# Head-by-head value loads, sums by head pair, and dummy products in the start of a fused attention and gated feed-forward kernel

## The chip, the cores and the metric

One core of one Trainium2 chip. The metric is the time of one execution on the device in microseconds (us), the median of several runs. A profiled run also gives the span, from the first to the last instruction that the trace holds; it is 1.7 us shorter than the run's time in most runs, and up to 2.6 us in a few. PE is the TensorE matrix engine, DVE is VectorE, ACT is ScalarE, POOL is GpSimd; "PEld" is PE's weight load. The granted clock of PE is 1.00 at full rate and 0.50 at half rate; in these traces it takes only these two values, so anything between is an average over a stretch.

Every ratio below is the mean time of one kernel's fast runs over that of the kernel before in the same rounds, so it is not quite the ratio of the medians quoted beside it.

## The reference

```python
batch, n_heads, seq, head_dim = 4, 8, 768, 64
k_sum = k.reshape(B, H, 24, 32, D).max(axis=3)       # one key for each block of 32
v_sum = v.reshape(B, H, 24, 32, D).mean(axis=3)      # one value for each block
# softmax over: keys nearer than 16 positions, and the 24 block keys (+ log 32)
x = softmax_scores @ concat(v, v_sum)                # -> 3072 tokens x 512
g = x @ w_gate                                       # 512 x 1536
ffn = (gelu(g) * (x @ w_val)) @ w_out
out = x + sigmoid(x @ w_res) * ffn
```

## The kernel before: the parts that the change touches

The work is cut into eight units (half a batch element each, 384 tokens). A unit computes scores (`s_step`: PE products, Exp on ACT, mask on DVE), value products (`av_step`: PE, reciprocal and scaling on DVE), transposes (`xt_step`: PE, copy on ACT or DVE), then twelve pairs of gate and value products (`fo_step`: PE, Gelu on ACT, product on DVE), then the output (`res_step`, `ffn_step`, `end_step`). The attention of unit u+1 is woven into the output of unit u, so only the attention of unit 0 has nothing to hide behind. The instruction order on each engine is the order of the program.

`vext` holds the values: rows 0 to 95 a window of positions, rows 96 to 127 the block means, which are products with an averaging matrix.

```python
def v_loads(b):                       # 12 loads, one window of all 8 heads each
    for t in range(NT):
        r0, r1, src = v_window(b, t)
        nc.gpsimd.dma_start(out=vext[b % 2][r0:r1, t, :, 0:D], in_=src)
# ... setup, k, q and v loads, then at once all weight loads on POOL's queue ...

for hp in range(3):
    k_step(0, hp, ps_mm, "mm")
# ... fourth key pair, first two query pairs
s_step(0, 0, st)
q_step(0, 0, 2, ps_mm, "mm")
vsum_mm(0, vs, 0, 3)                  # block means of ALL heads, window by window
s_step(0, 1, st)
# ... s_step 2 and 3, vsum_mm up to NT
nc.vector.tensor_copy(vsum[0][96:128, 0:DM // 2], vs[0][96:128, 0:DM // 2])
# ... copies of the means into vext on DVE, ACT, POOL
keep_warm(2)                          # dummy 128x128 products, 512 columns
av_step(0, 0, st)
keep_warm(2)
av_step(0, 1, st, ps_mm, "mm")
# ... xt_step and av_step in turn
g0, v0 = mm_tile("g"), mm_tile("vv")
gv_mm(g0, w_gate, st, 0, (0, 1))      # gate/value products begin
# ...
gv_end(gvT, 0, g0, v0)                # first Gelu

for u in range(NU):
    for fo in range(0 if u else 2, FO):
        fo_step(st, gvT, fo)
        if u == 0 and fo >= 8:
            q_step(0, 1, fo - 8, ps_t, "t")
        if u == 0 and fo == 10:       # first Exp of unit 1, amid the Gelus of unit 0
            nst = new_unit()
            s_step(1, 0, nst)
    # ... first_out: output of unit 0 with the rest of unit 1's attention
```

The softmax here doesn't subtract the row's maximum and nothing guards it: scores larger than these inputs give would overflow.

## Time and profile before

| | before |
|---|---|
| time, median of its first 3 runs | 282.56 us |
| span of the profiled run | 281.2 us |
| PE busy | 260.4 us, 93% |
| first keys landed, PE starts | 6.4 us |
| first value product | 21.55 us |
| steady gate/value products from | 29.36 us |
| first product of unit 1 | 60.60 us |

The page of the profile: the span, PE's busy time, and the busy share of PE in 40 slices of 7 us, in tenths.

```profile
span 281.2 us, 5757 instructions
...
PE   0799996999999999999899999999899999999994
...
PE 83%; DVE 6%; ACT 4%; issue 3%; DMA 3%; POOL 0%; POOLq 0%; DVEq 0%
```

The last line is the chain of work that ended last, by engine. PE is the limit nearly everywhere. A change that leaves PE's work alone can gain in the first two slices and in slice 7, where PE is not full, and wherever PE is full only because it runs at half rate, which this page does not show.

The timeline of the start of the kernel before (start, duration, engine, line, operation, what is written and read, how many; in brackets the idle time before and who ended it):

```profile
13.07 1.46 PE L241 MATMUL vs<-vext,bmat 96*32 96x256 bf16 x6
...
20.77 1.00 DVE L247 COPY vext<-vsum 32x768 bf16<-32x768 bf16 x2
...
21.55 0.54 PE L294 MATMUL ao<-vext,P 128*64 128x65 bf16 x12
...
25.23 0.42 PE L294 MATMUL ao<-vext,P 128*64 128x65 bf16 x12
...
27.53 1.28 ACT L321 ACT_TABLE_LOAD   x1
...
28.82 0.87 ACT L321 ACTIVATE ge<-g 128x384 f32<-128x384 f32 x2
...
29.36 0.81 PE L316 MATMUL g<-xT,w_gate 128*128 128x384 bf16 x4 [0.42 <-ACT ge L321]
```

The means are built over 7 us and copied before the first value product. Twelve value products take 0.54 us, and from 25.2 us on 0.42 and then 0.38: PE ran at half rate until about 25 us.

The same view of the middle, where the first Exp of unit 1 stands among the Gelus of unit 0:

```profile
42.85 1.28 ACT L280 ACT_TABLE_LOAD   x1
...
44.14 0.90 ACT L280 ACTIVATE P<-s,bias_t 128x768 bf16<-128x768 f32 x1
45.06 1.28 ACT L321 ACT_TABLE_LOAD   x1
...
45.09 0.35 PE L276 MATMUL s<-qT,kW 64*128 64x64 bf16 x12 [0.81 <-ACT P L280]
...
47.23 1.28 ACT L280 ACT_TABLE_LOAD   x1
...
49.48 0.35 PE L276 MATMUL s<-qT,kW 64*128 64x64 bf16 x12 [1.89 <-ACT P L280]
```

ACT loads the Exp table, the Gelu table and the Exp table again, and PE waits 0.81 and 1.89 us for it.

### The profile page before, as it was taken

How to read it: one execution, taken by the hardware profiler on the slowest of the kernel's cores; microseconds unless marked ns; L12 is line 12 of the kernel's file. 1: busy time of each engine (PE TensorE's matmuls, PEld its weight loads, DVE VectorE, ACT ScalarE, POOL GpSimd, SP SyncE). 2: the span in 40 equal slices, each digit the busy share in tenths (PEclk: the TensorE clock that was granted, in tenths of full speed). 3: DMA queues.
4: the chain of work that ended last, by engine and by line, in shares of the span. 5: the costliest groups of instructions: out<-in, count | busy, mean ns of one | idle time of the engine just before them, and what ended most of it. 6: DMA issues, size and time to landing. Idle time of an engine off the chain costs nothing.

```text
span 281.2 us, 5757 instructions
## 1 busy us (share of the span) xinstructions
PE 260.4 (93%) x2326; PEld 144.2 (51%) x2349; DVE 163.5 (58%) x366; ACT 131.9 (47%) x205; POOL 103.3 (37%) x130
## 2 busy tenths in 40 slices
PE   0799996999999999999899999999899999999994
PEld 0555553455555556455454555455455555456543
DVE  5965432489636734486866834575956733684424
ACT  1855549556473553652353434543254435444320
POOL 7995753600199982000899830000700000000000
PEclk9999999999999999999999999999999999999999
DMA  6999999991019999961099999421001100010003
GB/s 89 171 178 196 197 206 208 151 198 54 4 10 127 182 171 152 151 98 65 3 100 131 196 166 150 94 77 41 2 0 40 75 2 0 37 41 37 2 0 113
DMA packets 99818, 27.51 MB, mean 98 GB/s; under 512 B 83720, under 2 KB 96848, under 8 KB 99792
## 3 DMA queue, kind: packets, MB, share of 16 engines
q0 software_dynamic: 80560, 16.85, 68.4%
q1 hardware_dynamic: 19232, 10.30, 17.1%
q8 instruction: 18, 0.29, 0.4%
q14 instruction: 8, 0.07, 0.1%
HBM read 33.69 MB, written 6.29 MB: 142 GB/s over the span
## 4 chain that ended last, share of the span: by engine, by line
PE 83%; DVE 6%; ACT 4%; issue 3%; DMA 3%; POOL 0%; POOLq 0%; DVEq 0%
PE f L348 21%; PE g L316 20%; PE vv L316 19%; PE r L338 7%; PE ao L294 4%; PE s L276 3%; DMA q_sb<-in_q_dram 3%; PE xp L305 3%; DVE ks L207 2%; PE vs L241 2%; PE tp L233 2%; DVE gvT L322 2%; PE f L369 1%; ACT L280 1%; ACT L321 1%
## 5 line engine op out<-in xcount | busy, mean ns | idle before, releaser
L322 DVE TENSOR_TENSOR gvT<-ge,vv 128x384 bf16<-128x384 f32 x96 | 52.6, 552 | 58.9 <-PE vv L316 54.8
L321 ACT ACTIVATE ge<-g 128x384 f32<-128x384 f32 x96 | 47.0, 491 | 82.2 <-DVE gvT L322 43.7
L316 PE MATMUL vv<-xT,w_val 128*128 128x384 bf16 x384 | 78.4, 326 | 2.7 <-DVE gvT L322 2.7
L316 PE MATMUL g<-xT,w_gate 128*128 128x384 bf16 x384 | 79.9, 326 | 0.4 <-ACT ge L321 0.4
L348 PE MATMUL f<-w_out,gvT 128*128 128x512 bf16 x262 | 62.7, 379 | 1.4 <-issue 1.0
L316 PEld LDWEIGHTS <-w_val 128*128 128x128 bf16 x384 | 37.5, 98 | 28.7 <-issue 4.6
L316 PEld LDWEIGHTS <-w_gate 128*128 128x128 bf16 x384 | 35.8, 98 | 25.2 <-issue 3.0
L266 POOL COPY vext<-vsum 32x1536 bf16<-32x1536 bf16 x14 | 20.0, 1464 | 76.6 <-DMA vsum<-vpart 76.6
L280 ACT ACTIVATE P<-s,bias_t 128x768 bf16<-128x768 f32 x32 | 28.8, 901 | 30.6 <-PE s L276 30.5
L111 POOL DMA_DIRECT2D vext<-in_v_dram x48 | 36.5, 790 | 15.7 <-DMA w_out<-in_moe_w_out_dram 5.4
L348 PEld LDWEIGHTS <-gvT 128*128 128x128 bf16 x276 | 26.1, 98 | 29.1
L283 DVE TENSOR_TENSOR P<-P,maskt 128x768 bf16<-128x768 bf16 x32 | 17.7, 556 | 21.6 <-ACT P L280 21.6
L338 PE MATMUL r<-w_res,xT 128*128 128x512 bf16 x88 | 23.9, 381 | 0.4
L354 DVE SCALAR_TENSOR_TENSOR th<-th,f 128x512 f32<-128x512 f32 (+1 forms) x25 | 16.5, 659 | 6.4 <-PE f L348 6.1
L300 DVE TENSOR_TENSOR xn<-ao,rz 128x384 bf16<-128x384 f32 x32 | 17.8, 558 | 1.1
L119 POOL DMA_DIRECT2D k_nat<-in_k_dram x24 | 18.1, 771 | 0.0
L356 DVE SCALAR_TENSOR_TENSOR o<-th,xn 128x512 f32<-128x512 f32 (+1 forms) x25 | 16.8, 671 | 0.9
L298 DVE RECIPROCAL rz<-ao 128x6 f32<-128x6 f32 x32 | 6.2, 193 | 17.7 <-PE ao L294 17.7
L294 PEld LDWEIGHTS <-P 128*64 128x64 bf16 x384 | 9.0, 115 | 14.1 <-DVE P L283 5.5
L341 ACT ACTIVATE th<-r 128x512 f32<-128x512 f32 x24 | 14.2, 595 | 3.3 <-PE r L338 2.9
L207 DVE TENSOR_REDUCE ks<-kW 128x24 bf16<-128x768 bf16 x16 | 15.2, 948 | 0.3
L276 PE MATMUL s<-qT,kW 64*128 64x64 bf16 x384 | 11.8, 197 | 2.7 <-ACT P L280 2.7
(69 smaller groups left out, 188.4 us busy)
## 6 DMA issues: line engine op xcount, KB each, us to landing
out_dram<-o SPq DMA_DIRECT2D x23, 256.0 KB
vext<-in_v_dram POOLq DMA_DIRECT2D x40, 96.0 KB, 6.0
k_nat<-in_k_dram POOLq DMA_DIRECT2D x20, 96.0 KB, 3.7
q_sb<-in_q_dram POOLq DMA_DIRECT2D x4, 384.0 KB, 7.3
w_gate<-in_moe_w_gate_dram POOLq DMA_DIRECT2D x6, 256.0 KB, 8.2
w_val<-in_moe_w_val_dram POOLq DMA_DIRECT2D x6, 256.0 KB, 9.3
w_out<-in_moe_w_out_dram POOLq DMA_DIRECT2D x3, 512.0 KB, 14.3
q_nat<-in_q_dram POOLq DMA_DIRECT2D x12, 128.0 KB, 5.2
```

What stands on the lines that cost most here:

```text
L111: nc.gpsimd.dma_start(out=vext[b % 2][r0:r1, t, :, 0:D], in_=src)
L119: nc.gpsimd.dma_start(out=k_nat[r0:r0 + hi - lo, t].rearrange("p (h d) -> p h d", d=D), in_=k[b, :, lo:hi, :].rearrange("h p d -> p h d"))
L207: nc.vector.tensor_reduce(out=ks.rearrange("d (t n) -> d t n", n=2), in_=kw[:, :, WIN:WIN + QT].rearrange("d t (n w) -> d t n w", w=BLK), ...
L266: eng.tensor_copy(vext[b % 2][96:128, lo:hi, :, 0:D], src)
L276: nc.tensor.matmul(s[:, hh, t * QT:(t + 1) * QT], kw[ps, tt, hp, :], qt[ps, tt // 2, hp, (tt % 2) * QT:(tt % 2 + 1) * QT], start=True, sto ...
L280: nc.scalar.activation(P.rearrange("p a t q -> p a (t q)"), s[:, :, 0:TU], AF.Exp, scale=scale, bias=bias_t[:])
L294: nc.tensor.matmul(ao[64 * e:64 * e + 64, sub, hh, :], P[:, hh, t, :], vext[b % 2][:, half * HT + t, 2 * hp + hh, 0:D + 1], start=True, st ...
L316: nc.tensor.matmul(ps[:, 0:TU], w[:, ko, fo * 128:(fo + 1) * 128], st["xT"][:, ko, :], start=(ko == 0), stop=(ko == KO - 1), skip_group_ch ...
L321: nc.scalar.activation(ge[:], g[:, 0:TU], AF.Gelu)
L322: nc.vector.tensor_mul(gvT[:, fo, :], ge[:], vv[:, 0:TU])
L338: nc.tensor.matmul(r[:], st["xT"][:, ko, ss], w_res[:, ko, :], start=(ko == 0), stop=(ko == KO - 1))
L348: nc.tensor.matmul(st["f", sub][:], gvT[:, fo, ss], w_out[:, fo, :], start=(fo == 0), stop=(fo == FO - 1), skip_group_check=True)
```

## The change

Its intent: start unit 0's value products per head pair as soon as that pair's values have landed; release PE's clock early by dummy products; take the Gelu table load off the way; and move unit 1's first Exp behind the last Gelu. The diff, cut to its core:

```diff
 def v_loads(b):
-    for t in range(NT):
-        r0, r1, src = v_window(b, t)
-        nc.gpsimd.dma_start(out=vext[b % 2][r0:r1, t, :, 0:D], in_=src)
+    # first and last window for all heads (2 loads, cut here), then
+    for h in range(H):
+        src = bass.AP(tensor=v.tensor, offset=..., ap=[[D, BAND], [QT * D, NT - 2], [1, D]])
+        nc.gpsimd.dma_start(out=dst[0:BAND, 1:NT - 1, h, 0:D], in_=src)
@@ setup
+nc.vector.memset(warm[:], 0.0)            # first of all
-(memsets of vsum[1], bgrp, k_nat, kW[1])  # moved to behind xt_step(0, 2)
-(all weight loads)                        # now chunk by chunk: load_gv(c), load_rest()
+def vsum_pair(hp):
+    vs = ps_t.tile([128, 512], F32, tag="t", name="vs")
+    for t in range(NT):
+        nc.tensor.matmul(vs[96:128, 0:128], bmat[:, t, :], vext[0][0:BAND, t, 2 * hp:2 * hp + 2, 0:D], ...)
+    nc.scalar.copy(vsum[0][96:128, cols], vs[96:128, 0:128])
+    nc.gpsimd.tensor_copy(vext[0][96:128, 0:HT, 2 * hp:2 * hp + 2, 0:D], ...)
@@ start
+keep_warm(12)
 k_step(0, 0), k_step(0, 1)
+keep_warm(3)
 k_step(0, 2), fourth key pair
+keep_warm(4)
 q_step(0, 0, 0)
+keep_warm(2)
 q_step(0, 0, 1); s_step(0, 0); q_step(0, 0, 2); s_step(0, 1); q_step(0, 0, 3)
+vsum_pair(0); load_gv(1)
 s_step(0, 2); av_step(0, 0)
+vsum_pair(1); load_gv(2)
 s_step(0, 3)
+nc.scalar.activation(gate1[:], bias_t[0:1, :], AF.Gelu)     # loads the Gelu table
 xt_step(0, 0); av_step(0, 1)
+vsum_pair(2); load_gv(3)
 xt_step(0, 1); av_step(0, 2)
+vsum_pair(3); load_rest()
 xt_step(0, 2); keep_warm(2)
+(memsets of batch 1)
 gv_mm(g0, w_gate, st, 0, (0, 1)); av_step(0, 3); gv_mm(v0, ...); xt_step(0, 3); ...
@@ unit 0
-if u == 0 and fo == 10:
-    nst = new_unit()
-    s_step(1, 0, nst)
@@ first_out: s_step(n, 0) now leads, and the twelve ffn groups are spread anew (cut)
```

The copy of a sum takes two engines: ACT reads it out of PSUM, POOL spreads it. That follows the Trainium skill, "Trainium Kernel Development and Optimization", Key Constraints: POOL cannot access PSUM.

## The prediction

> **What bounds it now.** The page gives PE 93% busy over 281.2 us and 83% of the chain that ended last. From unit 1 on (60.6 us) PE's work is left alone, so only the first 60.6 us can move.
>
> There, by the timeline:
> - PE starts at 6.4 us, when the first keys land, and runs at half rate until about 25.1 us (12 products of the value step take 0.54 us, then 0.38).
> - Values are summed for all heads at once (PE 13.1 to 20.3 us), then copied into the value tile; the first value product waits until 21.55 us. The first Gelu follows at 28.82 us, behind a table load of 1.28 us; steady gate/value products start at 29.36 us.
> - From 29.36 to 60.60 us PE idles about 2.8 us: 0.81 and 1.89 us at 44.3 and 47.6 us, where unit 1's first Exp costs ScalarE two extra table loads (1.28 us each) amid the Gelus.
>
> By issue plus time to landing (DMA view), value loads land from 11.1 to 18.4 us, the last gate/value weights at 37.2 us, needed at 41.2 us.
>
> **What changes.**
> 1. Block sums, broadcast and value products go by head pair, the broadcast on POOL (32x1536 takes 1.46 us; estimate 0.73 us for a pair). The first value product moves to about 17 us. But each POOL copy stands between two weight issues of 0.77 us, so POOL's order sets the last copy: I estimate starts at 16.1, 18.4, 20.7 and 23.0 us. ScalarE's own chain (four key copies of 0.96, four query copies of 0.48, four Exps of 0.90 us, the query landing unchanged at 10.57) gives nearly the same beat.
> 2. The Gelu table load moves ahead of the transposed copies, off the chain: 1.3 us.
> 3. Setup memsets leave VectorE's early queue: about 1.1 us on its key chain.
> 4. Dummy products around the key transposes: PE warm by about 6.5 us.
> 5. Unit 1's first Exp moves behind the last Gelu: two table loads and 2.7 us of PE idle go; 28.4 us of work remain.
> 6. Value loads: 10 instead of 12, same bytes and 128-byte writes; no change in landing.
>
> **On the critical path.** If PE stays at full rate, gate/value work starts near 26.7 instead of 29.36 (2.6 us), plus 2.7 us from step 5: 5.3 us, unit 1 starting near 55.3. Weights (37.2 against a need at 38.3) still just arrive. That is 277.2 us.
>
> **The doubt.** The Trainium skill, "TensorE: Matmul & The Clock Gate", Part 1, says that a window of about 3.4 us of activity releases the clock and an idle one throttles it again. This trace shows that busy is not enough: from 12.2 to 20.3 us PE was full of small products (64-row, 32-column) and stayed at half rate. Between 11 and 22 us the changed kernel has just such products and no dummies. If the clock falls back there, PE's order becomes the limit (an estimated 2 to 4 us lost), leaving 279.5 to 281.
>
> **Predicted:** 278.0 us, range 276.4 to 281.0. Faster by over 2% 0.25, within 2% 0.73, slower 0.02.
>
> **What would show it.** Right: first value products near 17 us, 12 of them in 0.38 us; gate/value stream from 26 to 27 us; no PE gap over 1 us from 40 to 50 us; unit 1 near 55 us; the later span as before. Wrong: 0.54 us value products at 17 to 24 us (clock fell back); PE waiting on weight DMAs at 33 to 38 us; POOL copies much over 0.8 us.
>
> **Would make it wrong:** the clock state either way; POOL copies starving the weight DMAs; a much faster start, which the weights' arrival caps near 276 us.

## More of the kernel before

Busy time by stretches in the kernel before; the number after POOL's is the mean granted clock of PE:

```profile
core 0: us, PE busy (x) PEld busy (x) DVE busy (x) ACT busy (x) POOL busy (x), PEclk, DMA share, GB/s
15.00:18.40 3.40, 3.40 (x40) 1.99 (x42) 2.20 (x5) 2.17 (x3) 3.40 (x6) 1.00 2.14 166
```

Here one must read with care. The granted clock reads 1.00, but the products in this stretch have their half-rate durations. The clock's record begins only with the first release (at 25.4 us here); before it the column reads full. The durations of like products decide.

## The result, and the profile after

| | before | after |
|---|---|---|
| time, median of 4 runs each | 282.32 us | 281.78 us |
| ratio | | 0.9985 (0.9963 to 1.0006) |
| span of the profiled run | 281.2 us | 279.9 us |
| steady gate/value products from | 29.36 us | 30.05 us |
| first product of unit 1 | 60.60 us | 58.79 us |
| from the steady start to the end of the span | 251.8 us | 249.9 us |

The time is the same. The start is 0.7 us later, not 2.6 earlier, and the rest 1.9 us shorter. The profiled run of before was one of its longer ones (282.86 us against a median of 282.32), so the difference of the spans overstates that of the times.

The page after:

```profile
span 279.9 us, 5851 instructions
...
PE   8778999999999999999899999999899999999994
...
PEclk9965999999999999999999999999999999999999
```

The gap of slice 7 is gone. In slices 3 and 4 the granted clock is 0.6 and 0.5. The stretches:

```profile
core 0: us, PE busy (x) PEld busy (x) DVE busy (x) ACT busy (x) POOL busy (x), PEclk, DMA share, GB/s
13.20:16.60 3.40, 1.85 (x54) 1.61 (x54) 2.28 (x5) 3.11 (x6) 2.64 (x5) 1.00 2.51 155
16.60:20.00 3.40, 3.04 (x52) 2.48 (x48) 1.42 (x4) 1.51 (x3) 2.62 (x4) 0.51 2.07 178
...
23.50:26.90 3.40, 3.40 (x30) 2.03 (x28) 2.02 (x18) 0.74 (x2) 2.49 (x4) 0.50 1.46 195
26.90:30.30 3.40, 2.94 (x25) 1.66 (x22) 1.25 (x3) 1.35 (x3) 3.40 (x6) 1.00 1.44 194
```

The clock was released by the first dummies, fell back at 16.6 us after 3.4 us in which PE was busy only 1.85 us, and stayed at half for 10.2 us (16.65 to 26.89 us by the clock's record). The timeline of the start:

```profile
1.26 5.29 PE L376 MATMUL wp<-warm 128*128 128x512 bf16 x12 [1.26 <-DVE warm L150]
...
14.13 0.84 PE L242 MATMUL vs<-vext,bmat 96*32 96x128 bf16 x12
...
16.44 0.42 PE L293 MATMUL ao<-vext,P 128*64 128x65 bf16 x12 [1.18 <-POOL vext L246]
...
16.79 1.46 PE L242 MATMUL vs<-vext,bmat 96*32 96x128 bf16 x12
...
19.48 0.54 PE L293 MATMUL ao<-vext,P 128*64 128x65 bf16 x12 [0.36 <-POOL vext L246]
...
22.72 0.54 PE L293 MATMUL ao<-vext,P 128*64 128x65 bf16 x12 [0.87 <-POOL vext L246]
...
26.51 0.53 PE L293 MATMUL ao<-vext,P 128*64 128x65 bf16 x12
...
30.05 0.81 PE L315 MATMUL g<-xT,w_gate 128*128 128x384 bf16 x4
```

The first value products come at 16.44 us, 5 us sooner. But the sums of a pair then take 1.46 instead of 0.84 us, and a pair takes over 3 us, so the fourth pair's products come at 26.5 us. The same view further on, where unit 1 is prepared and begins:

```profile
45.24 1.28 ACT L279 ACT_TABLE_LOAD   x1
...
46.65 1.89 PE L347 MATMUL f<-w_out,gvT 128*128 128x512 bf16 x8
...
48.47 0.38 PE L293 MATMUL ao<-vext,P 128*64 128x65 bf16 x12
```

One table load is left, and PE works through it without a gap.

### The profile page after: what moved, and what is told of

Read it like the earlier page. It is cut to its first block, busy times and chain, and to the rows that moved or that the text cites. A ratio compares the mean times of both kernels' runs of the same rounds, so it can differ in the third digit from the quotient of the medians.

```text
span 279.9 us, 5851 instructions
## 1 busy us (share of the span) xinstructions
PE 266.5 (95%) x2391; PEld 146.0 (52%) x2391; DVE 161.7 (58%) x363; ACT 128.8 (46%) x205; POOL 102.0 (36%) x126
## 4 chain that ended last, share of the span: by engine, by line
PE 84%; DVE 5%; ACT 4%; DMA 3%; issue 2%; POOL 1%; POOLq 0%
PE g L315 21%; PE f L347 21%; PE vv L315 20%; PE r L337 8%; PE ao L293 4%; PE s L275 3%; DMA q_sb<-in_q_dram 3%; PE xp L304 2%; DVE ks L207 2%; PE tp L233 1%; DVE gvT L321 1%; ACT P L279 1%; PE vs L242 1%; PE vs L253 1%; PE f L368 1%
## 5 line engine op out<-in xcount | busy, mean ns | idle before, releaser
L347 PE MATMUL f<-w_out,gvT 128*128 128x512 bf16 x276 | 65.5, 379 | 0.0
L279 ACT ACTIVATE P<-s,bias_t 128x768 bf16<-128x768 f32 x32 | 28.9, 902 | 29.9 <-PE s L275 29.7
L111 POOL DMA_DIRECT2D vext<-in_v_dram x32 | 26.3, 854 | 11.1 <-DMA w_out<-in_moe_w_out_dram 5.1
L293 PE MATMUL ao<-vext,P 128*64 128x65 bf16 x384 | 12.7, 203 | 2.4 <-POOL vext L246 2.4
```

The lines of the kernel that those rows point to most:

```text
L111: nc.gpsimd.dma_start(out=dst[0:BAND, 1:NT - 1, h, 0:D], in_=src)
L279: nc.scalar.activation(P.rearrange("p a t q -> p a (t q)"), s[:, :, 0:TU], AF.Exp, scale=scale, bias=bias_t[:])
L293: nc.tensor.matmul(ao[64 * e:64 * e + 64, sub, hh, :], P[:, hh, t, :], vext[b % 2][:, half * HT + t, 2 * hp + hh, 0:D + 1], start=True, st ...
L347: nc.tensor.matmul(st["f", sub][:], gvT[:, fo, ss], w_out[:, fo, :], start=(fo == 0), stop=(fo == FO - 1), skip_group_check=True)
```

## The experiments

Fourteen kernels; all gave the right result. Each is told against the kernel before in the same rounds. The medians of the kernel before were 282.3 to 282.7 us. The changed kernel was not run again in these rounds, so a difference from it, or between kernels of different rounds (e1 to e4, e5 to e8, e9 to e11, e12 to e14), can be off by some tenths of a us.

### e2_second_alone: the second part on the old start

Edit: the kernel before, with the early `s_step(1, 0)` taken out and the new `first_out` put in.

> The kernel before with only the second part of the change: unit 1's first Exp moved behind the last Gelu, and the new order of the output step. If that part is worth what the idle of PE says (2.7 us): about 279.6 us. If, as the trace of the changed kernel suggests, about 0.7 to 1.4 us are given back where unit 1 begins (the last transposed copy comes later and delays the Gelu table load): 280.3 to 281.0 us, with the first 42 us as before.

Measured: 280.03 us, ratio 0.9915 (0.9889 to 0.9941). In the profile, steady start (28.64 us) to end of span takes 249.7 us, against 251.8 before: 2.1 us of gain. It is between the two expectations and slightly nearer the second, so a part of the gain is given back. That start of 28.64 us is 0.7 us earlier than in the profiled run of before, with the same code: the clock was released at 22.9 us here and at 25.4 us there, and the value products take 0.38 us from 22.97 us on here, while they still took 0.54 at 24.33 us there. So the steady start of the changed kernel is 0.7 to 1.4 us later than the old one.

### e3_start_alone: the new start with the old second part

Edit: the changed kernel with the old `first_out` and the early `s_step(1, 0)` put back.

> The changed kernel with the output step and the first Exp of unit 1 put back as before, so only the new start is left. Trace reading: the gate/value stream starts 0.7 us later than before because PE is at half rate from 16.9 to 27.1 us; so slower than before by about 0.5 to 0.9 us (282.8 to 283.2 us). If the start were the gain and the second part the loss: faster than before by 1 us or more.

Measured: 284.57 us, ratio 1.0069 (1.0041 to 1.0097): slower, by more than expected. The steady start is at 29.97 us as in the changed kernel. The surplus is a second fall of the clock, in the old gap. Busy time by stretches of e3_start_alone:

```profile
47.00:50.40 3.40, 1.51 (x30) 0.81 (x28) 0.88 (x2) 3.37 (x5) 0.82 (x1) 1.00 1.34 202
50.40:53.80 3.40, 3.40 (x12) 1.27 (x10) 1.46 (x4) 2.00 (x4) 1.97 (x3) 0.51 2.39 155
```

PE was busy 1.51 of 3.4 us, waiting for the table loads, and the next 3.4 us ran at half rate. If PE is the limit there, that costs about 1.7 us (an estimate: 3.4 x 0.5), which is the size of the surplus. But the same gap in the profiled run of the kernel before, with the same 1.51 us, brought no fall:

```profile
46.80:50.20 3.40, 1.51 (x29) 0.80 (x27) 1.26 (x4) 3.37 (x6) 0.77 (x1) 1.00 1.46 195
50.20:53.60 3.40, 3.40 (x27) 1.54 (x25) 1.07 (x2) 1.48 (x3) 2.21 (x3) 1.00 2.40 154
```

Counted in steps of 3.41 us from the clock's own changes, the emptiest window of that gap has 1.74 us there and 1.52 here; but the changed kernel fell after one with 1.90. So a gap makes a fall possible, not certain, and PE's busy share alone does not decide; what else does is not shown. All six runs have a mean granted clock of 0.973 to 0.976 (0.976 to 0.981 in the changed kernel); since the ranges touch, the means do not prove a second fall in every run. A fall of one such window costs 0.006 of the mean: 3.4 x 0.5 / 281. The kernel before shows the same deficit in some of its own runs: 11 of its 40 timed runs in all the rounds have a mean clock of 0.992 to 0.994, and these took 282.8 to 284.6 us. Where the clock fell in those is not shown, since they were not profiled. In e2_second_alone, without the gap, no run was below 0.999.

### e1_hold: dummies to hold the clock

```diff
+def hold(n):
+    wp = mm_tile("wp")
+    for _ in range(n):
+        nc.tensor.matmul(wp[:], warm[:, 0:128], warm[:], start=True, stop=True)
 q_step(0, 0, 2, ps_mm, "mm")
+hold(4)
 s_step(0, 1, st)
@@
 s_step(0, 2, st)
+hold(4)
 av_step(0, 0, st)
@@ and four each before av_step 1 and av_step 2
```

> The changed kernel plus 16 dummy 128x128 products of 512 columns, four at each of four places between 12 and 22 us where PE waits. Theory A (the clock falls back at 16.9 us for want of full-array products, and PE's order then limits the start): the granted clock stays at 1.0 from 6.6 us on, 12 value products take 0.38 and not 0.54 us, the gate/value stream starts about 2.5 us earlier (27.5 instead of 30.05 us), and the time falls to about 279.5 us. Theory B (POOL's order of copies and weight issues, or ScalarE's chain, sets the beat whatever the clock): the clock is held but the stream starts within 0.7 us of the changed kernel, and the time stays within 0.7 us of 281.8.

Measured: 279.97 us, ratio 0.9904 (0.9877 to 0.9931), so 1.8 us under the changed kernel by the medians. Busy time by stretches, and the timeline, of e1_hold:

```profile
13.20:16.60 3.40, 3.10 (x51) 1.87 (x50) 2.03 (x4) 3.12 (x6) 2.46 (x5) 1.00 2.51 154
16.60:20.00 3.40, 3.32 (x64) 2.42 (x64) 2.10 (x6) 2.15 (x4) 3.28 (x6) 1.00 1.99 180
```

```profile
19.18 0.38 PE L293 MATMUL ao<-vext,P 128*64 128x65 bf16 x12
...
20.95 0.26 ACT L244 CAST vsum<-vs 32x128 bf16<-32x128 f32 x1
...
26.32 0.34 PE L304 MATMUL xp<-ident,xn 128*128 128x128 bf16 x3 [0.97 <-DVE xn L299]
...
28.45 0.81 PE L315 MATMUL g<-xT,w_gate 128*128 128x384 bf16 x4
```

The clock stays at 1.00, value products take 0.38 us, and sixteen more products make the kernel faster. Theory A holds for the clock: filling the waits kept it at full rate. Rival B falls. But the steady start moves by 1.6 us, not 2.5. Even with the clock held it is at 28.45 us, where the prediction had 26.7. The lines show why. The third sum is ready on PE at about 20.3 us but is copied at 20.95, since the dummy Gelu with its table load stands ahead in ACT's order. And PE idles 0.97 us at the last transpose with ready products behind it.

### e5_tidy: three small moves in the start

```diff
-nc.scalar.activation(gate1[:], bias_t[0:1, :], AF.Gelu)   # ahead of xt_step(0, 0)
@@ behind xt_step(0, 2)
+nc.scalar.activation(gate1[:], bias_t[0:1, :], AF.Gelu)
-(memsets of batch 1)                                     # ahead of av_step(0, 3)
 av_step(0, 3, st)
+(two of them here, the rest behind the second Gelu)
 gv_mm(v0, w_val, st, 0, (0, 1))
-xt_step(0, 3, st, ps_t, "t", xcopy)
 gv_mm(g0, ..., (2,)); gv_mm(v0, ..., (2,)); gv_mm(g1, ..., (0, 1, 2))
+xt_step(0, 3, st, ps_t, "t", xcopy)
```

> e1_hold with three small moves in the start: the dummy Gelu (its table load) goes from before the first transposed copy to after the third; the setup memsets of batch 1 go from before the reciprocal of the last value products to after it; seven gate/value products go ahead of the last transpose, for which PE waited 0.97 us. Reading of e1_hold's trace (table load in ScalarE's order holds up the third sum's copy by 0.75 us, memsets hold up the last reciprocal by 0.6 us, PE idles 0.97 us): the stream starts near 26.8 instead of 28.45 us and the time falls by about 1.6 us, to 278.3 us. If something else sets the beat (weights' arrival, POOL): the stream starts after 28 us, or PE waits for weight DMAs later, and the time stays above 279.3 us.

Measured: 278.9 us, ratio 0.9861 (0.9838 to 0.9884). Timeline of e5_tidy:

```profile
20.22 0.26 ACT L244 CAST vsum<-vs 32x128 bf16<-32x128 f32 x1 [0.94 <-PE vs L242]
...
27.30 0.81 PE L315 MATMUL g<-xT,w_gate 128*128 128x384 bf16 x4
```

The third sum's copy comes 0.73 us earlier and the steady start 1.15 us earlier; 0.15 us of both was there already at the first value products (16.53 against 16.68 us), ahead of the moves. So about 1 us of the missing time lay in the order of instructions on ACT, DVE and PE. That is less than expected (26.8 us and 278.3 us). What each of the three moves is worth alone was not tried.

### e4_ahead: the sums one pair ahead, clock not held

Edit: in the changed kernel, `vsum_pair(1)` goes ahead of `av_step(0, 0)`, and so on.

> The changed kernel with the block sums of each head pair issued on PE one pair ahead of that pair's value products, no dummies added. Theory A with a serial loop (value products, then the next sums at half rate, then a ScalarE copy, a POOL copy, then the next value products, 3.1 us a turn): the turn shortens although the clock still falls back, the stream starts 1 to 1.5 us earlier, about 280.5 us. If only the rate of PE matters (PE full of work at half rate): less than 0.5 us. If POOL's issues set the beat: less than 0.5 us, with POOL busy without gaps from 15 to 24 us.

Measured: 281.72 us, ratio 0.9978 (0.9948 to 1.0008). This tells nothing of the serial loop: in the profiled run the half rate lasted from 13.6 to 30.6 us, and over its six runs the mean clock ranges from 0.967 to 0.988. The order changed what the clock did, and the two can't be parted.

### e8_ahead_held: the same with the clock held

Edit: e6_handoff (below) with the sums one pair ahead, the fourth pair's POOL copy ahead of a pair of weight issues, and the dummies spread anew.

> e6_handoff with the block sums one pair ahead of the value products and the fourth pair's POOL copy ahead of the fourth chunk's weight issues (dummies spread anew to hold the clock). If POOL's order (0.82 us a copy, 1.5 us the two issues between copies) is the next limit of the start: the last copy starts near 21.5 instead of 22.8 us, the stream up to 1 us earlier than in e6_handoff, about 276.4 us, unless the weights' arrival (last chunk near 37 us) then binds. If ScalarE's chain of copies and Exps is the next limit: within 0.4 us of e6_handoff.

Measured: 279.0 us, ratio 0.9863, against 279.2 for e6_handoff in the same rounds. The steady start is at 27.05 instead of 27.28 us. Within 0.4 us, so POOL's order is not the next limit of the start. That it is ACT's chain was the alternative, and is not shown by itself.

### e7_no_start_dummies: the shipped dummies taken out

```diff
-keep_warm(12)
@@ and keep_warm(3), keep_warm(4) and the first keep_warm(2)
```

> The changed kernel without its 21 dummy products before 11.5 us; the two before the gate/value products stay. If those dummies buy little as shipped, since the clock falls back at 16.9 us anyway: the stream starts 0 to 0.7 us later and the time is 281.8 to 282.5 us. If they carry the start: 283 us or more. Either way the granted clock is half up to about 27 us.

Measured: 282.79 us, ratio 0.9998 (0.9977 to 1.002). That is 1.0 us over the changed kernel by the medians and 0.4 by the ratios, whose intervals overlap. It is between the two expectations. The steady start is at 31.34 us, 1.3 later; the value products take 0.54 us up to the last at 27.36 us, and the clock is released only at 29.7. So in the profile the start dummies earn 1.3 us even though the clock falls back; in the time, a gain is likely but not clear of the noise.

### e11_tile_loads: the old value loads in the new order

Edit: e5_tidy with the old `v_loads`.

> e5_tidy with the value loads put back to one window of all heads after another. If the loads by head carry the head-pair order: the first sums on PE wait for the last load (18.4 us) instead of starting at 14.4 us, the stream starts 2 to 3 us later, about 281 us. If the sums had slack: under 0.5 us.

Measured: 284.62 us, ratio 1.007 (1.0041 to 1.01): 5.7 us over e5_tidy, twice what was expected. Timeline of e11_tile_loads:

```profile
17.17 0.22 PE L243 MATMUL vs<-vext,bmat 96*32 96x128 bf16 x1 [1.70 <-DMA vext<-in_v_dram]
...
21.71 0.54 PE L294 MATMUL ao<-vext,P 128*64 128x65 bf16 x12
```

The sums of the first pair wait window by window for loads until 19 us, and after that idle time (PE is busy 0.88 us from 15.86 to 19.27) the clock falls too (the first value products take 0.54 us; mean clock 0.988 to 0.993). In this order, sums by pair are worth nothing without loads by head.

### e6_handoff and e9_spread: the beginning of unit 1

In the changed kernel the steady start to unit 1's first product takes 28.74 us instead of 31.24, so 2.5 us less, but to the first table load of unit 1's output only 1.8 us less. The two kernels look for the other 0.7 us. Edits: e6_handoff puts a dummy Gelu and the last value products ahead of the first end step; e9_spread finishes the first row block of the output early, so that fewer end steps pile up.

> e5_tidy with the hand-over to unit 1 mended: the last value products of unit 1 and their scaling go ahead of the first end step on VectorE, one product of the output step goes behind the last transpose, and a dummy Gelu brings the table load to ScalarE's idle time before the last two transposed copies. Theory (the late transposed copy plus the table load behind it delay the Gelu of unit 1, and VectorE's key chain of unit 1 follows from it): unit 1's first Gelu comes about 1.2 us earlier relative to the stream's start and the time falls by about 1 us more, to 277.2 us. If VectorE's chain is set by something else: under 0.4 us.

Measured: 279.2 us, ratio 0.9871; 0.3 us over e5_tidy. The theory falls: unit 1's first Gelu started as early as hoped, but the three end steps, about 4.1 us in a row on DVE, then stood ahead of everything else there.

> e5_tidy with the output step of unit 0 reordered so that its first row block is finished early (as soon as the last third of w_out lands, near 47.5 us) and only the last block's end step is left for the hand-over, plus the dummy Gelu ahead of the last two transposed copies. Theory (e6_handoff's trace: the three end steps, 4.1 us on VectorE in a row, hold up the first Gelu product and key copy of unit 1): the first key copy on VectorE comes near 58.7 instead of 59.4 us and the time is 278.2 us. If ScalarE's table load and copies set it, as e6_handoff supposed: no gain over e5_tidy (278.9 us).

Measured: 278.69 us, ratio 0.9854 (0.9829 to 0.9879), 0.2 us under e5_tidy, which is not clear of the noise. The first key copy on DVE comes at 59.09 us, where 58.7 was expected for the theory and e5_tidy has 59.41; 0.2 us of that is the earlier steady start (27.10 against 27.30). It waits 0.32 us for ACT's key copy, as it did in e5_tidy (0.29). So that the end steps were part of it is not shown; the 0.7 us is open but for what the last section has.

### e10_narrow, e12_narrow_all, e13_narrow_short: what holds the clock

The prediction had read the kernel before so that the worked area of the array counts. Edits to the dummies of e1_hold: e10_narrow makes the sixteen holding ones 32 columns wide; e12_narrow_all makes all of them so, the releasing ones too; e13_narrow_short takes 96 rows as well, the shape of the sums.

```diff
-nc.tensor.matmul(wp[:], warm[:, 0:128], warm[:], start=True, stop=True)
+nc.tensor.matmul(wp[0:32], warm[0:96, 0:32], warm[0:96], start=True, stop=True)   # e13
```

> e1_hold with the 16 dummies at the four places made 32 columns wide instead of 128 (the same 512-column stream, so the same time on PE). If the clock follows how much of the array works: it falls back in the start as in the changed kernel, the 12 value products take 0.54 us, time 281.8 us or a little more. If it follows PE's busy time: it is held and the time is that of e1_hold, 280.0 us.

> e10_narrow with all dummies, also the 21 before 11.5 us that release the clock, 32 columns wide (128 rows, 512 columns streamed). If columns do not count: released at about 6.5 us as before, held, time 279.9 us. If releasing needs more of the array than holding does: half rate until full products come at 24 us or later, no release before, time 282.5 us or more.

> All dummies 96 rows by 32 columns, the shape of the sums that did not release the clock in the kernel before. If rows or area count: no release before the gate/value products, time 282.5 us or more. If only PE's share of busy time counts: released at about 6.5 us and held, 279.9 us; then the kernel before stayed at half rate from 12 to 20 us for another reason, which stays open.

Measured: 279.9, 279.92 and 279.91 us, ratios 0.9893, 0.9909 and 0.9909. All three are e1_hold's time, with the clock released before the first transposes and held. (One run of e13_narrow_short took 290.17 us and is not among the fast ones.) For these dummies neither rows nor columns count; a stream of 512-column products does it. Why the kernel before stayed at half rate through 8 us of small products is then left open. Its sums have the same 96 x 32 shape, with 256 columns each, and PE reads as busy all the time.

### e14_best: both parts that helped

Edit: the start of e8_ahead_held with the output step of e9_spread.

> The start of e8_ahead_held with the output step of e9_spread. If the two gains add: 0.2 us under e9_spread, 278.5 us. If the hand-over's VectorE chain or the weights' arrival now binds: no change from 278.7 us.

Measured: 278.51 us, ratio 0.9858 (0.9842 to 0.9875); span 276.6 us. By the medians it is 0.2 us under e9_spread, by the ratios not (0.9858 against 0.9854), so that the small gains add is not shown. It beats both kernels, and stays 2.5 us above the 276 us at which the prediction saw the weights' arrival as a cap.

## Why the prediction was wrong, point by point

- **The clock: the doubt, given too little weight.** The prediction named it and gave the case a cost of 2 to 4 us, but kept 278.0 us as its middle. The step that failed is "if PE stays at full rate, gate/value work starts near 26.7": PE was at half rate from 16.6 to 26.9 us, and that work started at 30.05 us. Holding the clock gains 1.8 us (e1_hold), so the fall itself cost no more than the doubt had said. That the time still lies 0.8 us above the upper end of 281.0 comes from the other terms below.
- **The start at full rate was mis-sized as well.** With the clock held the stream starts at 28.45 us, not 26.7. The prediction followed POOL's order and a chain on ACT, but left out what else stands in each engine's order: ready products behind a waiting transpose, a copy behind the table load. Moving three things gives 27.30 us (e5_tidy). Of the 3.35 us between 26.7 and 30.05, 1.6 went with the clock and 1.15 with e5_tidy; the last 0.6 is open.
- **Step 2, the table load "off the chain: 1.3 us".** It left one place and stood in the way of the next, by about 0.6 us once the clock was held (the third sum of e1_hold, ready at 20.3 us and copied at 20.95).
- **Step 3** was about right, as far as it can be told from step 4: the first key reduction on DVE starts at 8.47 us instead of 9.42.
- **The reason for the doubt does not hold for the fall.** That busy is not enough for a release still stands unexplained in the kernel before. Read as rows and columns of the array, it is contradicted for the dummies by e10_narrow to e13_narrow_short. Waits in PE's stream were what the fall followed: 1.85 us busy of 3.4 in the changed kernel, 1.51 in e3_start_alone. Filling them held the clock, but a gap of the same size in the kernel before brought no fall, so no threshold comes out of this.
- **Step 5** (2.7 us) was nearly right: 2.1 us in the profile of e2_second_alone, 2.3 us by its median. It also takes away a gap after which the clock can fall (e3_start_alone), which the prediction did not see.
- **Step 4** was right as far as 6.5 us: the key transposes from 6.48 us on are at full rate. The dummies are worth 1.3 us of the steady start and 0.4 to 1.0 us of the time (e7_no_start_dummies).
- **Step 1:** 16.44 us for the first value products (17 predicted), 0.82 us for POOL's copy (0.73 estimated). The copies of e1_hold start at 15.80, 18.19, 21.27 and 23.66 us (16.1, 18.4, 20.7 and 23.0 predicted).
- **Step 6:** taken for neutral, the loads by head carry the whole new order (e11_tile_loads, 5.7 us with the clock's part).
- **The weights did not bind:** neither the changed kernel nor the faster ones show PE waiting for their DMAs.

So the changed kernel adds a start that is 0.7 to 1.4 us later to a second part that is about 2 us shorter. In the four timed runs 0.5 us is left of it, not clear of zero.

## What to carry to other kernels

When serial work is cut into small pieces so that the first piece starts sooner, PE's stream gets gaps, and gaps can cost its clock: check the granted clock for the whole stretch, and fill the gaps with dummy products if it falls. A sum of durations along a dependency chain is too good by what stands ahead in each engine's own order; walk that order, engine by engine. And when a stage has a wait of about 2 us on PE, count the risk of a slow window after it, not the wait alone.

## What the Trainium skill lacked or had wrong

- "TensorE: Matmul & The Clock Gate", Part 1, has in its table of the two states that the clock is re-throttled after an idle window of about 3.4 us; it also tells of a kernel whose short idles made the clock swing, without saying how much idle time it takes. Here it fell after windows in which PE was busy 1.85 and 1.51 of 3.4 us, and did not fall after another with 1.51 (kernel before). The length of the window agrees: the stretches at half rate were 3.4 us (e3_start_alone) and 10.2 us, three of them (changed kernel).
- The same page has the clock released by a busy window of that length. In the kernel before, PE was busy 3.40 of 3.40 us from 15.0 to 18.4 us with short products and was not released, while twelve 512-column products, also of 96 rows by 32 columns, did release it (e13_narrow_short). The page sets only transposes apart (Part 4), which take 0.4 us of this stretch; which other products count, no page says.
- No page says that the granted clock in a trace reads full before its first record: 1.00 at 15 us in the kernel before, with half-rate durations, and a mean of 0.999 to 1.000 over the runs of e7_no_start_dummies, whose profiled run was not released before 29.7 us.
- "ScalarE: Activation LUTs", What ACT_TABLE_LOAD costs, gives about 2.66 us for a switch of tables, half of it a drain. Here the load takes 1.28 us, as the page has it, and no drain shows: an Exp ends at 45.04 us, the load runs from 45.06, and the Gelu starts at 46.35 us.
- No page has the price of many loads for one reader: the twelve mean products of batch 1 take 1.15 us with loads by head and 0.83 with loads by window (e5_tidy 1.14, and 0.83 in e11_tile_loads, which differs from it in the loads alone). The trace of e5_tidy shows ten semaphore waits of 51 ns in PE's weight queue over all batches, in place of one in e11_tile_loads.
